# Scratch tensors of a recurrent attention kernel kept in partition order, and the values of each head part projected next to its weighted sum

## The chip, the cores and the metric

One NeuronCore of one Trainium2 chip runs the whole program. The metric is the device time of one execution in microseconds (us); lower is better. Engines are named as in the profile: PE is TensorE's matmul, PEld is TensorE's weight load, DVE is VectorE, ACT is ScalarE, POOL is GpSimd, SP is SyncE, which here issues the transfers.

## The reference, cut to what matters

Forward and all gradients of a layer: a layer norm, an MLP with a squared relu, and an attention that runs over 64 segments of 32 tokens, each with 8 memory rows in front. The memory that goes into a segment is the attention output of the segment before, so 64 forward steps and then 64 backward steps follow each other and cannot overlap.

```python
def _A_ref(x, mem0, Wq, Wk, Wv, Wo, seg_len):       # x 1x2048x512, 32 heads of 128, 8 memory rows
    mem = mem0
    for s in range(n_seg):                          # seg_len 32
        h = concatenate([mem, x[:, s*seg_len:(s+1)*seg_len]], axis=1)
        q, k, v = einsum('btd,dhe->bhte', h, Wq), ...Wk, ...Wv
        p = softmax(where(mask, einsum('bhqe,bhke->bhqk', q, k) * scale, -1e9))
        o = einsum('bhqk,bhke->bhqe', p, v)
        o = einsum('bhte,hed->btd', o, Wo)
        mem = o[:, :M]                              # the next segment needs this
        outs.append(o[:, M:])
# result: x + A(layernorm(x)) + B(layernorm(x)), and its gradients for grad_out
# ... (layer norm, MLP B and the inputs left out)
```

A segment has 8 + 32 rows. The kernel carries 32 of them (the 8 memory rows and 24 tokens) through the recurrent steps. The other 8 tokens of a segment, whose attention outputs no later segment needs, are projected beforehand and finished in a batched "left" stage of 16 blocks of four segments.

## The kernel before

The program has five stretches, one after the other: MLP and projections of the left rows; 64 forward steps; 16 left blocks; 64 backward steps (four to a block, with extra work at a block's end); the weight gradients ("tail"). The stages hand each other their results through scratch tensors in DRAM. On chip a step's tensors have 128 partitions: four head groups g of 32 rows each. In DRAM most of them were kept by row, with the group inside:

```python
# S 2048, D 512, P 128, DC 4, HG 4 head groups, KH 8 heads each, GW = KH*P = 1024, SEG 32, M 8, NB 16, SPB 4
PARTS = ((0, 3), (3, 3), (6, 2))                       # the heads of a group, in three parts
S_NA = dram.tile([NB, HG, SPB, SEG, 3, GW], BF16, name="S_NA")
S_O = dram.tile([NROW, HD], BF16, name="S_O")
S_G = dram.tile([NROW, 3, HD], BF16, name="S_G")
S_RB = dram.tile([NROW, D], F32, name="S_RB")
# ...
def to_rows(t, r0):
    return t[r0:r0 + 32].rearrange("r (g c) -> g r c", g=HG)

def gather(R, XT, W, ks, first, last):                 # back from heads to 512 columns
    for k in ks:
        for g in range(HG):
            for c in range(DC):
                nc.tensor.matmul(R[32 * c:32 * c + 32, 0:P], lhsT=XT[:, k, g, :],
                                 rhs=W[:, g * KH + k, c * P:(c + 1) * P],
                                 start=(first and k == ks[0] and g == 0),
                                 stop=(last and k == ks[-1] and g == HG - 1), tile_position=(0, 32 * c))

def spill_nat(gTs, r0, copies):                        # a step's gradients of q, k, v to DRAM
    i = 0
    for t, gX in gTs:
        gN = wk.tile([P, GW], BF16, name="gNat", tag="gNat")      # this pool has two buffers of a tag
        for k0 in range(0, KH, 4):
            ps = trp.tile([P, 1024], BF16, name="ps_nat", tag="tr")
            for k in range(4):
                transpose_to(ps[:, k * P:(k + 1) * P], gX[:, k0 + k])
            copies[i % len(copies)](gN[:, k0 * P:(k0 + 4) * P], ps[:, 0:512])
            i += 1
        dma(S_G[r0:r0 + 32, t, :].rearrange("r (g c) -> g r c", g=HG), gN[:])
```

A forward step:

```python
for part in PARTS:
    # ... keys and queries projected, turned, scores, softmax, turned weights ET
for part in PARTS:
    proj(N3[:, 2], hT, Wqkv, 2 * HD, part, act_copy)              # the values, copied out by ACT
R = pbig("ps_R")
for i, part in enumerate(PARTS):
    k0, nk = part
    rs = norm(sts[i], L, Pb, part)
    weigh(ETs[i], rs, ((32, N3[:, 2]), (M, vLs)), part, ON)       # weighted sum of the values
    flip(OT[:, k0:k0 + nk], ON, part, act_copy)
    gather(R, OT, Wo, range(k0, k0 + nk), i == 0, i == len(PARTS) - 1)
Rb = ...                                                          # the next step's memory rows
# ... stores of the step: Rf, Rb, N3 into S_NA, ON into S_O and others
```

The left stage reads back the keys and values of the memory rows, and the backward step ends with its stores:

```python
kvM = ls.tile([P, 2, GW], BF16, name="l_kvM", tag="l_kvM")
dma(kvM[:].rearrange("p t c -> p (t c)"),
    S_NA[b].rearrange("g j r t c -> (g j) r (t c)")[:, 0:M, GW:3 * GW])
# ...
def rest(...):                                   # runs under the next backward step
    dma(to_rows(S_RB, s * SEG), Rf[:])
    dma(to_rows(S_MBB[s], 0), Rb[:])
    spill_nat(((2, gv), (1, gk), (0, gq)), s * SEG, (dve_copy, act_copy))
    if j == 0:                                   # last step of a block
        left_done(b, gkL, gvL)                   # three more gathers and another spill_nat
        finish_back(b)                           # loads S_RB rows back, row arithmetic, output rows
```

## Time and profile before

The median of three runs was 5192.39 us (5183.79 to 5195.74). I cut the profiled execution (span 5179.3 us) at four events: the first scores of the forward, the first use of `l_kvM` in the left stage, the first weight load of `b_QK` in the backward, and the last one; the stage lengths in every table below are first-to-last times of such an event, and the short joints between stages are left out. (The prediction cut the stages at their borders instead, so its levels are a little longer; its differences can be compared.)

| stage | us | PE busy, us | granted clock | DMA share |
|---|---|---|---|---|
| forward | 1043.5 | 901 | 0.97 | 0.39 |
| left | 419.8 | 191 | 0.63 | 0.52 |
| backward | 2073.4 | 1407 | 0.75 | 0.28 |
| after the last backward step | 655.3 | 574 | 0.93 | 0.49 |

These come from the table of stretches of the kernel before. Its columns are the stretch and its length, then busy time and instruction count of PE, PEld, DVE, ACT and POOL, then the granted TensorE clock, the DMA share (of 16 engines) and GB/s.

```profile
882.00:1925.00 1043.00, 901.39 (x25539) 538.59 (x25537) 490.96 (x1710) 443.65 (x1269) 180.39 (x502) 0.97 0.39 127
1986.00:2406.00 420.00, 191.09 (x6630) 127.16 (x6634) 157.63 (x398) 75.25 (x169) 40.97 (x63) 0.63 0.52 158
2451.00:4524.00 2073.00, 1407.09 (x49934) 1089.65 (x49932) 617.64 (x2538) 443.58 (x1575) 69.73 (x106) 0.75 0.28 87
4524.00:5179.00 655.00, 573.86 (x3106) 265.99 (x3094) 7.66 (x22) 80.24 (x145) 3.56 (x3) 0.93 0.49 169
```

In the backward PE is idle for a third of the time and its clock is low. Why it is idle stands in the list of waits of the kernel before over the whole span (engine, line, what it waited for: us in total, times, longest us):

```profile
DVE gNat L383 <- DMA S_G<-gNat: 718.3, 111, 10.7
...
ACT gNat L380 <- DMA S_G<-gNat: 520.2, 98, 9.4
...
PE ps_tr L179 <- DVE gNat L383: 310.1, 48, 8.3
```

The chain of waits in order of time shows one such place in a step (start us, us, what):

```profile
3206.96 0.33 PE ps_nat L179 x4
3207.29 0.13 PE ps_proj L402
3207.42 10.64 DMA S_G<-gNat
...
3218.18 0.43 DVE gNat L383
```

Three stores of a step share two buffers. The copy of the third needs the buffer of the first, and that store is still running; PE stands behind the copy. The same list for PE alone, in the backward (2451 to 4524):

```profile
PE ps_tr L179 <- DVE gNat L383: 310.1, 48, 8.3
PE ps_gR L485 <- issue: 77.8, 86, 2.5
...
PE ps_gkq L509 <- issue: 52.4, 46, 3.5
PE ps_gRL L485 <- issue: 46.0, 32, 2.0
```

"issue" is idle time in which PE waited for nothing that the profile shows: 176.2 us here.

### The profile page before, as it was taken

How to read it: one execution, taken by the hardware profiler on the slowest of the kernel's cores; microseconds unless marked ns; L12 is line 12 of the kernel's file. 1: busy time of each engine (PE TensorE's matmuls, PEld its weight loads, DVE VectorE, ACT ScalarE, POOL GpSimd, SP SyncE). 2: the span in 40 equal slices, each digit the busy share in tenths (PEclk: the TensorE clock that was granted, in tenths of full speed). 3: DMA queues.
4: the chain of work that ended last, by engine and by line, in shares of the span. 5: the costliest groups of instructions: out<-in, count | busy, mean ns of one | idle time of the engine just before them, and what ended most of it. 6: DMA issues, size and time to landing. Idle time of an engine off the chain costs nothing.

```text
span 5179.3 us, 196279 instructions
## 1 busy us (share of the span) xinstructions
PE 3590.4 (69%) x89874; PEld 2270.7 (44%) x89874; DVE 1515.1 (29%) x5110; ACT 1225.2 (24%) x3450; POOL 312.3 (6%) x741
## 2 busy tenths in 40 slices
PE   3940658888888882444666766666666666649999
PEld 1520224555555541322555555555555555524444
DVE  5520003444444442333232332323322233300000
ACT  1310024444444431111222222222222222201111
POOL 0000000111111110000000000000000000000000
PEclk8975989999999995666777777777777877769999
DMA  4377564344433346555222222222222222255553
GB/s 141 121 174 211 164 230 160 123 131 132 133 130 129 126 149 222 154 163 167 81 89 87 88 88 89 88 90 90 90 86 88 89 85 86 71 165 188 193 182 123
DMA packets 457504, 672.89 MB, mean 130 GB/s; under 512 B 159817, under 2 KB 257762, under 8 KB 454370
## 3 DMA queue, kind: packets, MB, share of 16 engines
q1 hardware_dynamic: 456674, 660.34, 40.2%
q8 instruction: 702, 11.50, 0.9%
q14 instruction: 128, 1.05, 0.1%
HBM read 349.84 MB, written 289.94 MB: 124 GB/s over the span
## 4 chain that ended last, share of the span: by engine, by line
PE 53%; DMA 28%; DVE 6%; ACT 5%; issue 4%; SPq 3%; POOL 1%; DVEq 0%; POOLq 0%; ACTq 0%
DMA S_G<-gNat 13%; PE ps_gR L485 11%; PE ps_proj L402 9%; PE ps_gw L953 8%; PE ps_tr L179 5%; PE ps_R L485 4%; PE ps_gwo L966 3%; PE ps_gkq L509 2%; DMA l_kvM<-S_NA 2%; PE ps_wgh L470 2%; DVE ON L475 1%; DMA S_WT<-wtt 1%; ACT OT L380 1%; PE ps_nat L179 1%; PE ps_sc L426 1%
## 5 line engine op out<-in xcount | busy, mean ns | idle before, releaser
L402 PE MATMUL ps_proj<-Wqkv,hT 128*32 128x384 bf16 x9216 | 474.4, 312 | 0.5 <-ACT hT L634 0.3
L383 DVE COPY gNat<-ps_nat 128x512 bf16<-128x512 bf16 x240 | 101.9, 425 | 797.9 <-DMA S_G<-gNat 718.3
L485 PE MATMUL ps_gR<-WT_39551,gk 128*32 128x128 bf16 x8192 | 239.1, 275 | 125.2 <-DVE gk L383 66.1
L953 PEld LDWEIGHTS <-HNc 128*128 128x128 bf16 x1920 | 188.4, 98 | 295.1 <-issue 70.3
L179 PE MATMUL ps_tr<-ident,gON 128*128 128x128 bf16 x512 | 82.8, 294 | 310.7 <-DVE gNat L383 310.1
L380 ACT COPY gNat<-ps_nat 128x512 bf16<-128x512 bf16 x240 | 140.5, 586 | 603.9 <-DMA S_G<-gNat 520.2
L402 PEld LDWEIGHTS <-hT 128*32 128x32 bf16 x9216 | 210.4, 96 | 97.9 <-issue 4.1
L485 PE MATMUL ps_gR<-WT_39549,gv 128*32 128x128 bf16 x8192 | 243.9, 293 | 6.2 <-issue 5.2
L485 PEld LDWEIGHTS <-gk 128*32 128x32 bf16 x8192 | 178.2, 122 | 157.3 <-DVE gk L383 68.5
L380 ACT CAST gk<-ps_gkq 128x192 bf16<-128x192 f32 (+1 forms) x256 | 70.2, 274 | 738.1 <-PE ps_gkq L509 738.1
L402 PE MATMUL ps_proj<-WoT,goT 128*32 128x384 bf16 (+1 forms) x3072 | 205.7, 352 | 23.3 <-POOL goT L799 23.0
L485 PE MATMUL ps_gR<-WT_48287,gq 128*32 128x128 bf16 x8192 | 197.9, 262 | 24.9 <-issue 24.1
L485 PEld LDWEIGHTS <-gv 128*32 128x32 bf16 x8192 | 201.3, 132 | 25.1 <-ACT gv L859 13.6
L383 DVE CAST gk<-ps_gkq 128x192 bf16<-128x192 f32 (+1 forms) x256 | 72.9, 285 | 433.8 <-PE ps_gkq L509 433.7
L485 PE MATMUL ps_R<-Wo,OT 128*32 128x128 bf16 x8192 | 153.9, 231 | 58.7 <-ACT OT L380 55.6
L485 PEld LDWEIGHTS <-gq 128*32 128x32 bf16 x8192 | 172.9, 121 | 35.5 <-issue 34.3
L179 PEld LDWEIGHTS <-gON 128*128 128x128 bf16 x512 | 42.3, 117 | 318.5 <-issue 309.1
L470 PEld LDWEIGHTS <-ET 32*32 32x32 bf16 (+1 forms) x5120 | 84.9, 100 | 193.7 <-issue 184.8
L485 PEld LDWEIGHTS <-OT 128*32 128x32 bf16 x8192 | 128.3, 103 | 84.0 <-ACT OT L380 78.8
L470 PE MATMUL ps_wgh<-l_kvM,ET 32*32 32x128 bf16 x512 | 30.2, 300 | 166.1 <-DMA l_kvM<-S_NA 164.1
L345 PE MATMUL ps_w_2827<-ghn,xnN 128*128 128x512 bf16 x16 | 6.5, 405 | 190.2 <-DMA ghn<-S_GH1N 190.2
L475 DVE TENSOR_TENSOR ON<-ps_wgh,sm_rs 128x384 bf16<-128x384 f32 (+1 forms) x192 | 92.6, 510 | 149.6 <-PE ps_wgh L470 149.5
(952 smaller groups left out, 7047.2 us busy)
## 6 DMA issues: line engine op xcount, KB each, us to landing
S_G<-gNat SPq DMA_DIRECT2D x240, 256.0 KB
b_QK<-S_NA SPq DMA_DIRECT2D x64, 512.0 KB
S_VTA<-vT SPq DMA_DIRECT2D x64, 320.0 KB
b_vT<-S_VTA SPq DMA_DIRECT2D x64, 320.0 KB
S_O<-ON SPq DMA_DIRECT2D x64, 256.0 KB
ghn<-S_GH1N SPq DMA_DIRECT2D x32, 448.0 KB
an<-S_AN SPq DMA_DIRECT2D x32, 448.0 KB
S_WT<-wtt SPq DMA_DIRECT2D x48, 256.0 KB
```

Of the source, the lines that this page charges most:

```text
L179: nc.tensor.transpose(ps_ap, in_ap, ident[base:base + k, base:base + k])
L345: nc.tensor.matmul(pss[k][:, :nf], lhsT=xnN[:, rc, dc * P:(dc + 1) * P], rhs=ghn[:, f0g:f0g + nf], start=(rc == 0), stop=(rc == TC - 1),)
L380: nc.scalar.copy(out, in_)
L383: nc.vector.tensor_copy(out, in_)
L402: nc.tensor.matmul(ps[32 * g:32 * g + 32, 0:nk * P], lhsT=hT[:, dc, :], rhs=W[:, dc, c:c + nk * P], start=(dc == 0), stop=(dc == DC - 1), ...
L426: nc.tensor.matmul(sc3[32 * g:32 * g + 32, k, c:c + n], lhsT=qT[:, k0 + k, g, :], rhs=kT[:, k0 + k, g, :], start=(mask is None), stop=True ...
L470: nc.tensor.matmul(ps[32 * g:32 * g + 32, k * P:(k + 1) * P], lhsT=ET[32 * g:32 * g + n, k, i, :], rhs=V[32 * g:32 * g + n, (k0 + k) * P:( ...
L475: nc.vector.tensor_tensor(out=dst[:, k0 * P:(k0 + nk) * P].rearrange("p (k e) -> p k e", k=nk), in0=ps[:, 0:nk * P].rearrange("p (k e) -> ...
L485: nc.tensor.matmul(R[32 * c:32 * c + 32, 0:P], lhsT=XT[:, k, g, :], rhs=W[:, g * KH + k, c * P:(c + 1) * P], start=(first and k == ks[0] a ...
L509: nc.tensor.matmul(out(ps[g], k), lhsT=N_[32 * g:32 * g + m, k * P:(k + 1) * P], rhs=X(k)[32 * g:32 * g + m], start=first, stop=last, tile ...
L953: nc.tensor.matmul(ps[:], lhsT=HNc[:, rc, dc * P:(dc + 1) * P], rhs=gn[:, rc, u * 512:(u + 1) * 512], start=(rc == 0), stop=(rc == RC_ALL ...
L966: nc.tensor.matmul(ps[:], lhsT=on[:, rc, i * P:(i + 1) * P], rhs=GOc[:, rc, :], start=(rc == 0), stop=(rc == RC_ALL - 1))
```

## The change

There are two independent intents. First, the scratch tensors are stored in partition order, so that both sides of a step's transfer have 128 as their outer dimension. The author counted on transfers spread over more DMA engines, and "the spread" means these layouts. With it, the three stores of a step's gradients become one of 768 KB from a larger tile, with still two buffers (so with two steps of slack); the rows of a block are finished later; two pairs of tiles share a tag to make room. Second, in the forward each part's values are projected directly before the weighted sum that uses them, instead of all three parts before the first.

```diff
-    S_NA = dram.tile([NB, HG, SPB, SEG, 3, GW], BF16, name="S_NA")
+    S_NA = dram.tile([NSEG, HG, SEG, 3, GW], BF16, name="S_NA")
-    S_O = dram.tile([NROW, HD], BF16, name="S_O")
-    S_G = dram.tile([NROW, 3, HD], BF16, name="S_G")
+    S_O = dram.tile([NSL, HG, SEG, GW], BF16, name="S_O")
+    S_G = dram.tile([NSL, HG, SEG, 3, GW], BF16, name="S_G")
     ... (S_MBF, S_MBB, S_RF, S_RB likewise; loads and stores adapted)
-        def spill_nat(gTs, r0, copies):
+        def spill_nat(gTs, sl, copies):
             i = 0
+            gN = wk.tile([P, 3, GW], BF16, name="gNat", tag="gNat")
             for t, gX in gTs:
-                gN = wk.tile([P, GW], BF16, name="gNat", tag="gNat")
     ...
-                dma(S_G[r0:r0 + 32, t, :].rearrange("r (g c) -> g r c", g=HG), gN[:])
+            dma(S_G[sl].rearrange("g r t c -> (g r) t c"), gN[:])
     ...
-            for part in PARTS:
-                proj(N3[:, 2], hT, Wqkv, 2 * HD, part, act_copy)
             R = pbig("ps_R")
             for i, part in enumerate(PARTS):
                 k0, nk = part
+                proj(N3[:, 2], hT, Wqkv, 2 * HD, part, act_copy)
                 rs = norm(sts[i], L, Pb, part)
     ...
-            dma(kvM[:].rearrange("p t c -> p (t c)"),
-                S_NA[b].rearrange("g j r t c -> (g j) r (t c)")[:, 0:M, GW:3 * GW])
+            for g in range(HG):
+                dma(kvM[32 * g:32 * g + 32].rearrange("p t c -> p (t c)"),
+                    S_NA[b * SPB:(b + 1) * SPB, g].rearrange("j r t c -> j r (t c)")[:, 0:M, GW:3 * GW])
     ...
                 if j == 0:
                     left_done(b, gkL, gvL)
-                    finish_back(b)
+                if j == 1 and b < NB - 1:
+                    finish_back(b + 1)
     ... (after the loop: finish_back(0); tags of two tile pairs merged;
         the weight gradients load each block as four quarters)
```

More of the change, by code (lines that the diff above doesn't have):

```diff
@@ L114 @@
     S_XN = dram.tile([S, D], BF16, name="S_XN")
-    S_MBF = dram.tile([NSEG, SEG, D], BF16, name="S_MBF")
-    S_MBB = dram.tile([NSEG, SEG, D], BF16, name="S_MBB")
+    NSL = NSEG + NB
+    S_MBF = dram.tile([NSEG, DC, SEG, P], BF16, name="S_MBF")
+    S_MBB = dram.tile([NSEG, DC, SEG, P], BF16, name="S_MBB")
     S_XNT = dram.tile([P, DC, S], BF16, name="S_XNT")
@@ L131 @@
     S_GQL = dram.tile([NB, P, KH, HG, NL], BF16, name="S_GQL")
-    S_O = dram.tile([NROW, HD], BF16, name="S_O")
-    S_G = dram.tile([NROW, 3, HD], BF16, name="S_G")
-    S_RF = dram.tile([NROW, D], F32, name="S_RF")
-    S_RB = dram.tile([NROW, D], F32, name="S_RB")
+    S_O = dram.tile([NSL, HG, SEG, GW], BF16, name="S_O")
+    S_G = dram.tile([NSL, HG, SEG, 3, GW], BF16, name="S_G")
+    S_RF = dram.tile([NSL, DC, SEG, P], F32, name="S_RF")
+    S_RB = dram.tile([NSL, DC, SEG, P], F32, name="S_RB")
     S_WT = dram.tile([P, 3, H, D], BF16, name="S_WT")
@@ L386, in any_copy @@
         nc.any.tensor_copy(out, in_)
-    def to_rows(t, r0):
-        return t[r0:r0 + 32].rearrange("r (g c) -> g r c", g=HG)
     def make_ops(big, trp, scp, wk, sm):
@@ L521, in spill_nat @@
                         transpose_to(ps[:, k * P:(k + 1) * P], gX[:, k0 + k])
-                    copies[i % len(copies)](gN[:, k0 * P:(k0 + 4) * P], ps[:, 0:512])
+                    copies[i % len(copies)](gN[:, t, k0 * P:(k0 + 4) * P], ps[:, 0:512])
                     i += 1
-                dma(S_G[r0:r0 + 32, t, :].rearrange("r (g c) -> g r c", g=HG), gN[:])
+            dma(S_G[sl].rearrange("g r t c -> (g r) t c"), gN[:])
         return pbig, proj, flip, scores, softmax, norm, turn, weigh, gather, dscores, outer, spill_nat
     def fetch_rows(dst, src, b):
-        dma(dst[:], src[b * P:(b + 1) * P, :])
         for j in range(SPB):
-            r0 = AROWS + b * NL + M * j
-            dma(dst[32 * j:32 * j + M, :], src[r0:r0 + M, :])
+            d3 = dst[32 * j:32 * j + 32, :].rearrange("r (c d) -> r c d", c=DC)
+            dma(d3[M:SEG], src[b * SPB + j].rearrange("c r d -> r c d")[M:SEG])
+            dma(d3[0:M], src[NSEG + b].rearrange("c r d -> r c d")[M * j:M * j + M])
     wo_cm = sb("wo", 1, "right")
@@ L647, in rest @@
                 nc.gpsimd.tensor_copy(TM[:, 1, :, :, lc], vT[:, :, :, 0:M])
-                dma(to_rows(S_RF, s * SEG), Rf[:])
-                dma(to_rows(S_MBF[s], 0), Rb[:])
-                dma(S_NA[b, :, j], N3[:])
+                dma(S_RF[s].rearrange("c r d -> (c r) d"), Rf[:])
+                dma(S_MBF[s].rearrange("c r d -> (c r) d"), Rb[:])
+                dma(S_NA[s].rearrange("g r t c -> (g r) t c"), N3[:])
                 dma(S_VTA[s], vT[:])
                 dma(S_PA[s], Pb[:])
-                dma(to_rows(S_O, s * SEG), ON[:])
+                dma(S_O[s].rearrange("g r c -> (g r) c"), ON[:])
                 if j == SPB - 1:
@@ L701 @@
                 gather(R, OT, Wo, range(k0, k0 + nk), k0 == 0, k0 + nk == KH)
-            dma(to_rows(S_O, AROWS + b * NL), ON[:])
+            dma(S_O[NSEG + b].rearrange("g r c -> (g r) c"), ON[:])
             Rf = ld.tile([P, P], F32, name="l_Rf", tag="l_Rf")
             nc.any.tensor_copy(Rf[:], R[:, 0:P])
-            dma(to_rows(S_RF, AROWS + b * NL), Rf[:])
+            dma(S_RF[NSEG + b].rearrange("c r d -> (c r) d"), Rf[:])
             goT = ld.tile([P, DC, NL], BF16, name="goTL", tag="goTL")
@@ L759, in left_done @@
         def left_done(b, gkL, gvL):
-            gqL = bt.tile([P, KH, HG, NL], BF16, name="gqLb", tag="gqLb")
+            gqL = bt.tile([P, KH, HG, NL], BF16, name="gqLb", tag="acc4")
             dma(gqL[:], S_GQL[b])
@@ L766, in left_done @@
             nc.any.tensor_copy(Rf[:], R[:, 0:P])
-            dma(to_rows(S_RB, AROWS + b * NL), Rf[:])
-            spill_nat(((2, gvL), (1, gkL), (0, gqL)), AROWS + b * NL, (dve_copy, act_copy))
+            dma(S_RB[NSEG + b].rearrange("c r d -> (c r) d"), Rf[:])
+            spill_nat(((2, gvL), (1, gkL), (0, gqL)), NSEG + b, (dve_copy, act_copy))
         def finish_back(b):
@@ L791, in finish_back @@
                                     op0=ALU.add, op1=ALU.mult)
-            gib = bt.tile([P, D], BF16, name="gib4", tag="gib4")
+            gib = bt.tile([P, D], BF16, name="gib4", tag="xnb4")
             dma(gib[:], gflat[r0:r0 + P, :])
@@ L818 @@
             QK = bs.tile([P, 2, GW], BF16, name="b_QK", tag="b_QK")
-            dma(QK[:].rearrange("p t c -> p (t c)"), S_NA[b, :, j].rearrange("g r t c -> g r (t c)")[:, :, 0:2 * GW])
+            dma(QK[:], S_NA[s].rearrange("g r t c -> (g r) t c")[:, 0:2, :])
             kLs = bs.tile([P, GW], BF16, name="b_kLs", tag="b_kLs")
@@ L907, in rest @@
             def rest(s=s, b=b, j=j, gv=gv, gk=gk, gq=gq, Rb=Rb, Rf=Rf, gkL=gkL, gvL=gvL):
-                dma(to_rows(S_RB, s * SEG), Rf[:])
-                dma(to_rows(S_MBB[s], 0), Rb[:])
-                spill_nat(((2, gv), (1, gk), (0, gq)), s * SEG, (dve_copy, act_copy))
+                dma(S_RB[s].rearrange("c r d -> (c r) d"), Rf[:])
+                dma(S_MBB[s].rearrange("c r d -> (c r) d"), Rb[:])
+                spill_nat(((2, gv), (1, gk), (0, gq)), s, (dve_copy, act_copy))
                 if j == 0:
                     left_done(b, gkL, gvL)
-                    finish_back(b)
+                if j == 1 and b < NB - 1:
+                    finish_back(b + 1)
             later.append(rest)
@@ L916 @@
             f()
+        finish_back(0)
     bw_cm.__exit__(None, None, None)
-    dma(out2flat[:, :], S_MBB[0][0:M, :])
+    dma(out2flat.rearrange("r (c d) -> r c d", c=DC), S_MBB[0].rearrange("c r d -> r c d")[0:M])
     with tc.tile_pool(name="p5", bufs=2) as p5, tc.tile_pool(name="p5b", bufs=1) as p5b, \
@@ L925, in slot_side @@
             dma(t_[:, 0:TC, :], src.rearrange("(c p) d -> p c d", p=P))
-            sv = smem[:].rearrange("(b j) r d -> j r b d", j=SPB)
+            sv = smem[:].rearrange("(b j) c r d -> j c r b d", j=SPB)
             for j in range(SPB):
@@ L930, in slot_side @@
                 b0, b1 = max(0, -o), min(NB, NB - o)
-                dma(t_[32 * j:32 * j + M, b0:b1, :], sv[jj, 0:M][:, b0 + o:b1 + o, :])
+                for c in range(DC):
+                    dma(t_[32 * j:32 * j + M, b0:b1, c * P:(c + 1) * P], sv[jj, c, 0:M][:, b0 + o:b1 + o, :])
             if lo < 0:
@@ L942 @@
         GOc = slot_side("GOc", gflat, S_MBB, zeros_bf[:], 1)
-        CW = 1024
+        CW = GW
         for t, outW in enumerate((out_3, out_4, out_5)):
@@ L947 @@
                 gn = p5.tile([P, RC_ALL, CW], BF16, name="gn5", tag="gn5")
-                dma(gn[:], S_G[:, t, c0:c0 + CW].rearrange("(c p) n -> p c n", p=P))
+                for j in range(SPB):
+                    dma(gn[32 * j:32 * j + 32], S_G[:, c0 // CW, :, t, :].rearrange("(b j) r c -> j r b c", j=SPB)[j])
                 for dc in range(DC):
@@ L961 @@
             on = p5.tile([P, RC_ALL, CW], BF16, name="on5", tag="gn5")
-            dma(on[:], S_O[:, c0:c0 + CW].rearrange("(c p) n -> p c n", p=P))
+            for j in range(SPB):
+                dma(on[32 * j:32 * j + 32], S_O[:, c0 // CW].rearrange("(b j) r c -> j r b c", j=SPB)[j])
             for i in range(CW // P):
```

## The prediction

> **What bounds it now.** The table of engines by stretch gives: MLP and left projections to 880 us; 64 forward steps, 1077 us (PE busy 911, granted clock 0.96); 16 left blocks, 466 (PE 199, clock 0.62); 64 backward steps, 2147 (PE 1434, clock 0.75); weight gradients, 609 (PE 555). The chain of waits puts 13% (690 us) on stores S_G<-gNat, all in the backward: 8 to 10 us a step, 6 more per block, and 6 to 7 us for an S_RB load. The list of waits agrees: DVE 718, ACT 520 us before gNat. Three 256 KB stores share two gNat buffers; the third waits for the first. Backward DMA is busy 0.29 of 16 engines: as if under five did all.
>
> [...]
>
> **Removed.** (a) [...]S_G becomes one 768 KB store per step with two steps of slack: its waits vanish. (b) A block's gradient rows are finished two steps later, off the chain: 6.5 us load plus 5 us POOL/DVE per block. Replaying one step (3076.8 to 3105.4 us) with its durations in the new instruction order, the first scores start near 3082.0, not 3089.6: 21 us instead of 28.6; the block-end step 32 instead of 45. That is 96 us per block, not 133. Without 6 us gaps PE's clock should rise from 0.75 towards 0.9 ([...]the clocks above agree), counted as 7 us: 89. PE's "issue" gaps inside gathers (176 us) stay. 16 x 44 = 700 us, plus 28 for four stacked stores at the end.
>
> **Added.** (c) Forward: PE's built order is now wgh0, turn, gather0, values 1, wgh1, values 2, turn, wgh2, gather1, turn, gather2; before, all values preceded wgh0, and wgh1/wgh2 followed gather0. PE now stands for the value copy (0.48 us ACT) before wgh0 and wgh1, and the last turn waits for a late wgh2. Replayed from the last scores to Rb: 7.5 us before, 9.8 now; ON0 still waits for DVE's softmax, so the move hides nothing. 2.3 x 64 = 145 us. (d) Left stage: kvM becomes four loads with an outer 4[...]. (e) 24 more small loads before the weight gradients: +12.
>
> **Prediction.** 5190 - 700 - 28 + 145 + 75 + 12 = about 4695 us; 8 in 10: 4480 to 4900. Faster by over 2%: 0.96; within 2%: 0.03; slower: 0.01.
>
> **What would show it.** S_G<-gNat gone from the chain and from DVE's and ACT's waits; backward near 1430 us at clock 0.85 to 0.92. Forward near 1220, PE waiting on ACT's value copy at wgh. Left stage near 540, l_kvM wait near 240.
>
> **What would make it wrong.** If issue gaps grow once no store wait hides them, the backward gains less (4900); if crowded DMA engines cause them, they shrink (4480). If the clock does not rise: +110. [...]If the forward's clock falls with its density, (c) grows.

The sum came to 5190 - 700 - 28 + 145 + 75 + 12 = 4694, about 4695 us. Without (d) the sum would be about 4620 us. The rise of the clock in (b) stands as the estimate from the clocks of the stages above: 0.62 where PE was busy for 199 of 466 us, 0.75 at 1434 of 2147, 0.96 at 911 of 1077. The 28 us of the stores at the end and the 12 us of (e) are estimates too; one of these loads takes 0.42 us to issue in the kernel after (median on SyncE).

## The result, and the profile after

| | before | after |
|---|---|---|
| median, us | 5194.07 (5183.79 to 5198.28, 4 runs) | 5069.13 (5066.16 to 5072.19, 4 runs) |
| span of the profiled run, us | 5179.3 | 5068.2 |
| granted clock, whole span | 0.820 | 0.844 |

The ratio is 0.9762 (95% interval 0.9745 to 0.9779): faster by 2.4%, where 9.6% was predicted, and outside the range. A ratio here and below is the mean time of one kernel's fast runs over that of the other's in the same rounds, so it is not quite the ratio of the quoted medians.

By stage, from first-to-last times of the same events:

| stage, us | before | after | difference | predicted |
|---|---|---|---|---|
| forward | 1043.5 | 1293.2 | +249.7 | +145 |
| left | 419.8 | 455.9 | +36.1 | +75 |
| backward | 2073.4 | 1666.0 | -407.4 | about -700 |
| after the last backward step | 655.3 | 672.4 | +17.1 | -16 (-28 and +12) |
| start and joints | | | -6.6 | 0 |

The sum is -111.1 us, the difference of the two spans. The table of stretches of the kernel after, columns as before, in the same order of stages:

```profile
886.00:2179.00 1293.00, 1045.46 (x25547) 585.44 (x25543) 486.35 (x1711) 463.78 (x1269) 180.65 (x502) 0.89 0.30 103
2237.00:2693.00 456.00, 203.65 (x6630) 131.13 (x6634) 158.00 (x397) 75.19 (x168) 41.23 (x63) 0.62 0.47 147
2730.00:4396.00 1666.00, 1347.29 (x49945) 1023.93 (x49944) 614.64 (x2540) 449.89 (x1576) 70.02 (x106) 0.85 0.34 107
4396.00:5068.00 672.00, 568.47 (x3030) 261.02 (x3078) 7.62 (x22) 81.48 (x145) 3.57 (x3) 0.95 0.78 164
```

The list of waits over the whole span, kernel after. The copies into `gNat` now wait for PE and no longer for a store:

```profile
DVE gNat L385 <- PE ps_nat L181: 308.9, 239, 11.6
...
ACT gNat L382 <- PE ps_nat L181: 140.9, 234, 1.6
```

So the store waits were really taken away, and the backward's clock did rise from 0.75 to 0.85. What PE waits for in the backward (2730 to 4396) is now led by lines that name no releaser:

```profile
PE ps_gR L484 <- issue: 114.5, 134, 2.4
PE ps_gkq L508 <- issue: 76.9, 59, 2.6
PE ps_gRL L484 <- issue: 49.5, 33, 3.4
```

These "issue" gaps grew from 176.2 to 240.9 us. They are not scattered. Here are the gaps of one backward step in PE's timeline, kernel after (start us, us, engine, line, instruction, output and inputs, count, then the idle time before it and its releaser):

```profile
3329.94 3.15 PE L484 MATMUL ps_gR<-WT_39549,gv 128*32 128x128 bf16 x109 [0.86 <-issue]
...
3333.96 0.17 PE L508 MATMUL ps_gkq<-gST,b_QK 32*128 32x32 bf16 x1 [0.47 <-issue]
...
3337.98 1.44 PE L484 MATMUL ps_gR<-WT_39551,gk 128*32 128x128 bf16 x45 [1.71 <-issue]
...
3342.00 0.59 PE L484 MATMUL ps_gR<-WT_48383,gq 128*32 128x128 bf16 x13 [0.41 <-issue]
```

The four starts lie 4.02 us apart. Counting the rows of the trace between them gives exactly 128 products each time, and every product comes with one weight load, so 256 PE instructions. That count does not depend on what the instructions are: the four gaps fall in front of different lines and tiles. Over the whole backward of this trace 232 idle times of PE over 0.15 us end with "issue", and each of the 231 distances between neighbours is a multiple of 128 products (up to two records missing in the trace).

What comes after every 256 instructions is, by three numbers, the supply of instructions itself: the period of 256; the line of an instruction queue on the page of the kernel after (shown below: packets, MB, share of 16 engines), with 702 packets and 11.50 MB, 16 KB each; and 702 times 256 = 179,712, against PE's 89,874 products and as many weight loads (179,748; that count is from the kernel before, and the queue's line has the same packets in both kernels). That the line is PE's shows in two runs below: e7, with some 45,400 PE instructions fewer, has 525 packets, 177 fewer, and e5, with some 7,200 more, has 731. So below, a block is 256 PE instructions, and a refill is the coming of the next one, as these numbers suggest. In the backward of this kernel the refills cost idle time. Where two such gaps follow each other after just one block, the median distance of their ends is 3.75 us (139 distances in the kernel after, mean 3.87, 10th to 90th percentile 3.47 to 4.30; 70 in the kernel before, median 3.74, mean 3.76, 3.47 to 4.02). That is about 68 PE instructions per us.

```profile
q8 instruction: 702, 11.50, 1.0%
```

From this follows a limit that the prediction did not have. The backward stretch holds 49,945 + 49,944 = 99,889 PE instructions, 390 blocks. At 3.75 us each that is 1463 us (an estimate worked out from the two numbers). The prediction's 700 us of gain amount to 2073 - 700 = 1373 us in this cut: below the limit. The limit is not in force all the time: the 139 blocks with a starved gap at both ends take 538 of the 1666 us, and the stage as a whole takes 4.27 us a block.

### The profile page after: what moved, and what is told of

It is laid out like the page before. It is cut to its first block, busy times and chain, and to the rows that moved or that the text cites. A ratio compares the mean times of both kernels' runs of the same rounds, so it can differ in the third digit from the quotient of the medians.

```text
span 5068.2 us, 195611 instructions
## 1 busy us (share of the span) xinstructions
PE 3680.1 (73%) x89788; PEld 2250.3 (44%) x89874; DVE 1507.3 (30%) x5110; ACT 1253.2 (25%) x3450; POOL 313.2 (6%) x741
## 3 DMA queue, kind: packets, MB, share of 16 engines
q8 instruction: 702, 11.50, 1.0%
## 4 chain that ended last, share of the span: by engine, by line
PE 59%; DMA 14%; issue 8%; DVE 8%; ACT 8%; SPq 3%; POOL 0%; ACTq 0%; POOLq 0%; DVEq 0%
PE ps_proj L401 11%; PE ps_gR L484 11%; PE ps_gw L956 7%; PE ps_tr L181 5%; PE ps_R L484 4%; PE ps_nat L181 3%; PE ps_gkq L508 3%; PE ps_gwo L970 3%; DMA l_kvM<-S_NA 2%; PE ps_gRL L484 2%; PE ps_wgh L469 2%; DVE ON L474 2%; ACT OT L382 2%; DMA S_WT<-wtt 1%; DMA ghn<-S_GH1N 1%
## 5 line engine op out<-in xcount | busy, mean ns | idle before, releaser
L401 PE MATMUL ps_proj<-Wqkv,hT 128*32 128x384 bf16 x9216 | 569.0, 349 | 0.6 <-ACT hT L581 0.3
L401 PEld LDWEIGHTS <-hT 128*32 128x32 bf16 x9216 | 223.1, 103 | 127.7 <-issue 36.9
L469 PEld LDWEIGHTS <-ET 32*32 32x32 bf16 (+1 forms) x5120 | 113.3, 104 | 315.1 <-issue 296.3
L484 PE MATMUL ps_gR<-WT_39549,gv 128*32 128x128 bf16 x8192 | 205.3, 255 | 29.0 <-issue 27.9
L484 PE MATMUL ps_R<-Wo,OT 128*32 128x128 bf16 x8192 | 170.7, 238 | 75.8 <-ACT OT L382 75.4
L484 PEld LDWEIGHTS <-gv 128*32 128x32 bf16 x8192 | 164.0, 115 | 44.4 <-issue 37.5
L469 PE MATMUL ps_wgh<-l_kvM,ET 32*32 32x128 bf16 x512 | 41.2, 299 | 192.3 <-DMA l_kvM<-S_NA 190.3
L508 PEld LDWEIGHTS <-b_QK 32*128 32x128 bf16 x4096 | 123.3, 93 | 93.6 <-issue 68.0
L382 ACT COPY OT<-ps_tr 128x384 bf16<-128x384 bf16 (+1 forms) x192 | 85.2, 444 | 212.2 <-PE ps_tr L181 208.2
```

Of the source, the lines that this page charges most:

```text
L382: nc.scalar.copy(out, in_)
L401: nc.tensor.matmul(ps[32 * g:32 * g + 32, 0:nk * P], lhsT=hT[:, dc, :], rhs=W[:, dc, c:c + nk * P], start=(dc == 0), stop=(dc == DC - 1), ...
L469: nc.tensor.matmul(ps[32 * g:32 * g + 32, k * P:(k + 1) * P], lhsT=ET[32 * g:32 * g + n, k, i, :], rhs=V[32 * g:32 * g + n, (k0 + k) * P:( ...
L508: nc.tensor.matmul(out(ps[g], k), lhsT=N_[32 * g:32 * g + m, k * P:(k + 1) * P], rhs=X(k)[32 * g:32 * g + m], start=first, stop=last, tile ...
```

## The experiments

Four questions were open. Is the backward now bound by the supply of PE instructions, or by the array and its clock? Was it the old layout of the stores or the wait for a buffer that cost the backward so much? Is the forward's loss the new order alone? And is the left stage's loss the `kvM` load? All experiments ran beside the kernel before on the same chip, in three groups. In the group of e1 to e4 its median was 5142.26 us (5134.98 to 5147.6), in that of e5 to e8 5167.38 (5159.26 to 5171.23), in that of e9 to e12 5187.49 (5177.78 to 5205.92), seven runs each. e4, e5 and e12 have one run each, whose state is unknown; their stage lengths are read for large differences only. Each row of the table is one profiled execution. The backward's code is the same in after, e1, e5 and e8, and its length there is 1632 to 1683 us, so a difference under some 50 us between two backwards is not read. Stage lengths of all runs, us:

| kernel | forward | left | backward | end | ratio to before |
|---|---|---|---|---|---|
| before | 1043.5 | 419.8 | 2073.4 | 655.3 | 1 |
| after | 1293.2 | 455.9 | 1666.0 | 672.4 | 0.976 |
| e1: after, values first | 1079.4 | 458.5 | 1632.1 | 669.1 | 0.934 |
| e2: before, values moved | 1294.0 | 418.1 | 2061.2 | 653.1 | 1.052 |
| e3: before, four buffers | 1039.9 | 419.6 | 1693.4 | 649.7 | 0.929 |
| e4: after, narrow gather | 1287.8 | 459.7 | 1706.6 | 672.1 | one run, 5087.01 us |
| e5: after, filled waits | 1235.8 | 459.9 | 1682.7 | 674.0 | one run, 5025.6 us |
| e6: after, old S_NA | 1293.7 | 406.9 | 1669.8 | 671.7 | 0.972 |
| e7: after, wide gather | 1294.6 | 463.7 | 1348.1 | 674.1 | 0.920 |
| e8: after, values between | 1021.8 | 452.7 | 1650.9 | 670.7 | 0.923 |
| e9: old layouts, rest of the change | 1043.6 | 418.1 | 1704.8 | 647.8 | 0.924 |
| e10: e9, wide, between | 1042.2 | 415.1 | 1521.1 | 645.2 | 0.889 |
| e11: e6, wide, between | 1019.3 | 401.1 | 1368.6 | 672.5 | 0.859 |
| e12: after, stores twice | 1293.8 | 455.8 | 1760.5 | 681.2 | one run, 5173.76 us |

### e1, e2: the order of the values alone

e1 takes the new order out of the kernel after; e2 puts it alone into the kernel before.

```diff
 # e1, on the kernel after (e2 is the reverse, on the kernel before)
+            for part in PARTS:
+                proj(N3[:, 2], hT, Wqkv, 2 * HD, part, act_copy)
             R = pbig("ps_R")
             for i, part in enumerate(PARTS):
                 k0, nk = part
-                proj(N3[:, 2], hT, Wqkv, 2 * HD, part, act_copy)
                 rs = norm(sts[i], L, Pb, part)
```

> The changed kernel with the forward's value projections all before the first weighted sum again, as before the change; all DRAM layouts of the change kept. Theory A (the moved projections cost the forward, 1062 us before, 1314 us changed; half by the waits of the new order, half by the lower clock those waits bring): the forward falls back to 1050-1080 us at granted clock about 0.96, and the whole run to 4800-4840 us. Rival B (the forward got slower by the new stores' layout): the forward stays above 1250 us and the total within 1% of 5069 us.

> The kernel before with only the value projections moved next to their weighted sum. Theory A: the forward grows by about 250 us to about 1310 us at clock about 0.88, total about 5440 us, the other stages as before. Rival B (layout): forward within 20 us of 1062 us, total within 1% of 5194 us. If only the waits of the order counted, as predicted, and not the clock: forward about 1210 us, clock 0.96.

e1, correct: 4804.23 us (4783.67 to 4824.64, 4 runs), ratio 0.9344 [0.9313, 0.9375]; the forward falls to 1079.4 us. e2, correct: 5408.19 us, ratio 1.0522 [1.0503, 1.0542]; the forward is 1294.0 us, +250 on layouts that were not touched. So the loss of the forward comes with the order of the values and not with the layouts: e2 has all of it on the old ones (the 36 us that e1 keeps over the kernel before are taken up under e9). Its clock falls with it; the forward stretches of e1 and then e2, columns as before:

```profile
875.00:1954.00 1079.00, 920.58 (x25539) 546.91 (x25531) 491.30 (x1711) 443.72 (x1269) 176.97 (x502) 0.95 0.36 123
```

```profile
873.00:2167.00 1294.00, 1046.06 (x25535) 585.59 (x25527) 487.25 (x1713) 463.10 (x1269) 181.80 (x502) 0.88 0.33 102
```

The same 25,535 products take PE 1046 us where they took 901 before: this is a slower clock, not only a longer wait. One step of the kernel after shows how that comes about. PE's idle times in it, from its timeline:

```profile
1504.46 0.23 PE L469 MATMUL ps_wgh<-N_21798,ET 32*32 32x128 bf16 x4 [0.39 <-ACT N_21798 L382]
...
1505.82 0.34 PE L181 MATMUL ps_tr<-ident,ON 128*128 128x128 bf16 x3 [0.65 <-DVE ON L474]
1506.73 1.22 PE L484 MATMUL ps_R<-Wo,OT 128*32 128x128 bf16 x48 [0.57 <-ACT OT L382]
...
1509.80 0.29 PE L469 MATMUL ps_wgh<-N_21798,ET 32*32 32x128 bf16 x4 [0.57 <-ACT N_21798 L382]
...
1514.74 0.28 PE L181 MATMUL ps_tr<-ident,ON 128*128 128x128 bf16 x2 [0.53 <-DVE ON L474]
```

`N` is the value tile: PE now stands for ACT's copy of it before a weighted sum, as predicted. And the same step in stretches (columns as before):

```profile
1504.00:1507.00 3.00, 1.40 (x49) 0.97 (x52) 1.43 (x7) 1.42 (x4) 0.96 (x3) 1.00 0.00 0
1507.00:1510.40 3.40, 2.83 (x84) 1.89 (x72) 0.00 (x0) 0.48 (x1) 0.00 (x0) 0.51 0.09 29
1510.40:1513.60 3.20, 3.13 (x82) 2.03 (x75) 0.56 (x1) 0.85 (x2) 0.61 (x2) 0.50 0.24 102
1513.60:1517.00 3.40, 1.98 (x64) 1.22 (x53) 0.72 (x2) 0.82 (x3) 0.00 (x0) 0.96 0.81 255
```

In the 3 us before 1507 PE is busy for 1.40 us, in short pieces; then the granted clock is 0.51 and 0.50 for 6.6 us, in which PE is nearly always busy, with work that takes up to twice as long: the groups of four `ps_wgh` products start 0.06 us apart from 1504.5 us on, at a clock of 1.00, and 0.11 us apart from 1509.9 us on. No single idle time in the step exceeds 0.65 us, so the clock fell here without any long gap. At which density of work it falls, no run shows.

### e5: the forward's waits filled with products that nobody reads

If the clock follows density, useless products in the waits should make the step shorter although work is added.

```diff
 # e5, on the kernel after
+        def fill(ps, n):
+            for _ in range(n):
+                nc.tensor.matmul(ps[:, 384:512], lhsT=ident[:], rhs=ident[:], start=True, stop=True,
+                                 skip_group_check=True)
...
                 weigh(ETs[i], rs, ((32, N3[:, 2]), (M, vLs)), part, ON)
+                fill(R, 14 if i < 2 else 8)
                 flip(OT[:, k0:k0 + nk], ON, part, act_copy)
+                fill(R, 7)
```

> The changed kernel, with idle spots of PE in the forward (after each weighted sum, after each turn, before the second and third weighted sum) filled by 128x128 products into unused columns of ps_R that nobody reads: some 64 more products a step, 3.7 us of array time. Theory F (of the 3.9 us that the moved values cost per step, about 2.3 are waits of the order and the rest is PE's clock, which the waits push to half speed): a forward step falls from 20.3 us to 18 to 19.3 us, granted clock from 0.88 to above 0.96, although work was added. Rival G (all of it is waiting in the new order): the step stays at 20.3 us or grows.

Correct; 5025.6 us in a single run (state unknown). The forward stretch, columns as before:

```profile
880.00:2116.00 1236.00, 1149.34 (x29129) 732.12 (x29122) 487.41 (x1714) 463.95 (x1270) 181.34 (x502) 1.00 0.31 108
```

The clock is 1.00 throughout and the forward is 57 us shorter, with 3,582 products more (some 56 a step). So a part of the loss is the clock. I had expected a larger gain: a quiet step took 19.56 us instead of 20.3, where 18 to 19.3 had been named. (The 3.7 us of array time for 64 products fit the trace of the kernel after, where each further product of a turn adds 0.06 us at a clock of 1.00: two take 0.28 us, three 0.34.) The filling lies on the chain itself in some places, so 57 us understates the clock's share. A better look is the part of a step that has neither a reordered instruction nor a filling, from Rb to the last scores of the next step: its mean is 8.63 us before (clock 0.99), 9.48 after (0.89) and 8.54 in e5 (1.00).

### e8: the values of the next part projected into the wait of this one

```diff
 # e8, on the kernel after
+            proj(N3[:, 2], hT, Wqkv, 2 * HD, PARTS[0], act_copy)
             R = pbig("ps_R")
             for i, part in enumerate(PARTS):
                 k0, nk = part
-                proj(N3[:, 2], hT, Wqkv, 2 * HD, part, act_copy)
                 rs = norm(sts[i], L, Pb, part)
                 weigh(ETs[i], rs, ((32, N3[:, 2]), (M, vLs)), part, ON)
+                if i + 1 < len(PARTS):
+                    proj(N3[:, 2], hT, Wqkv, 2 * HD, PARTS[i + 1], act_copy)
+                if i > 0:
+                    gather part i - 1
                 flip(OT[:, k0:k0 + nk], ON, part, act_copy)
-                gather part i
+            gather the last part
```

> The changed kernel with another place for the values: the next part's values projected right after a weighted sum, before its turn, and each gather one part later, so PE has work while ON and OT are made. The built order is wgh0, values 1, turn, wgh1, values 2, gather0, turn, wgh2, gather1, turn, gather2. Worked out from the step's durations: 1.0 to 1.5 us shorter than the 16.07 us of a quiet step before, so a step of 14.6 to 15.3 us at clock above 0.95, forward 950-990 us between its first and last scores (1293 in the changed kernel, 1079 with all values first), total ratio to before about 0.91 to 0.92.

Correct: 4767.28 us, ratio 0.9231 [0.9218, 0.9245]. The forward is 1021.8 us, 271 us less than after and 22 us less than before. The intent of moving the values (to give PE work while ON is computed) works if the values come one part ahead. The step was expected at 14.6 to 15.3 us and took 15.96: my expectation was too good, as PE was already busy for 13.86 of 16 us in a step of the kernel before, so little more was to be had.

### e3: four buffers, nothing else

This tells whether the old stores' layout or the wait for a buffer was the cost.

```diff
 # e3, on the kernel before
-                gN = wk.tile([P, GW], BF16, name="gNat", tag="gNat")
+                gN = wk.tile([P, GW], BF16, name="gNat", tag="gNat0" if t == 0 else "gNat")
```

> The kernel before with four gNat buffers instead of two (the third store of a step has its own pair)[...]. Theory C (only the wait for a buffer cost; what remains is PE's supply of instructions, 256 per 3.5 to 4.3 us when it runs dry): the gNat waits nearly vanish and the backward falls from 2130 to 1700-1800 us, about what the whole change got there, total 4770-4880 us. Rival D ([...]the spread was needed): the wait moves to other DMA (QK loads, S_RB) and the backward stays above 1950 us.

Correct: 4779.68 us (4773.42 to 4781.93), ratio 0.9292 [0.9277, 0.9308]. One line, with the old layouts and the stores untouched, gains three times as much as the whole change, which carries the forward's loss. The waits of the copies into `gNat` for a store fall from 1238 us (718.3 and 520.2 above) to 98. Its backward stretch, columns as before:

```profile
2437.00:4130.00 1693.00, 1322.78 (x49915) 1007.07 (x49918) 611.63 (x2540) 449.80 (x1576) 69.88 (x106) 0.85 0.33 106
```

It is 1693 us, 27 above the kernel after and 61 above e1 (the same backward code as after), at about the same clock. So most of the backward's gain came from the slack in buffers; the new layout of the stores was hardly needed for it.

### e4: a quarter of the array work, the same number of instructions

If the array or its clock bounds the backward, streaming 32 instead of 128 columns per gather product must help. If the instruction supply does, nothing changes.

```diff
 # e4, on the kernel after, backward only; gives a wrong result on purpose
+                    n = P if edge or not narrow else 32        # edge: first and last product
-                        nc.tensor.matmul(R[32 * c:32 * c + 32, 0:P], lhsT=XT[:, k, g, :],
-                                         rhs=W[:, g * KH + k, c * P:(c + 1) * P],
+                        nc.tensor.matmul(R[32 * c:32 * c + 32, 0:n], lhsT=XT[:, k, g, :],
+                                         rhs=W[:, g * KH + k, c * P:c * P + n],
```

> The changed kernel with the backward's gathers streaming 32 columns instead of 128 in all but the first and last products of each sum: the same instructions in the same order, a quarter of the array's work in 30,000 of them. Gives a wrong result on purpose. Theory C (instruction supply): backward within 6% of 1706 us (1600 to 1710), the issue gaps grow from about 243 us to above 400 us. Rival E (array time at the granted clock): each gather product drops by some 10 to 20 ns, backward below 1450 us, the gaps unchanged.

Wrong (relative error 0.84 in one of the outputs); 5087.01 us in one run. Backward stretch and PE's waits in it (2707 to 4413):

```profile
2707.00:4413.00 1706.00, 1153.49 (x49933) 810.79 (x49934) 611.15 (x2539) 452.75 (x1575) 70.04 (x106) 0.64 0.32 105
```

```profile
PE ps_gR L486 <- issue: 274.9, 179, 3.1
PE ps_gkq L511 <- issue: 137.9, 63, 3.1
PE ps_gRL L486 <- issue: 66.5, 32, 3.9
```

PE's busy time falls by 194 us (some 6.5 ns for each of the 30,000 products; the rival's 10 to 20 are an estimate, and three quarters of the 29 ns that a gather product takes in the step traced above, 109 in 3.15 us, would be 22) and its issue gaps grow by 238 us; the stage is no shorter (1706.6 against 1666.0). The 203 one-block distances between gap ends have a median of 3.74 us. The array's work was not what the backward waited for. The clock fell to 0.64; what that cost alone cannot be read here, because the array had less work at the same time.

### e7: the same work in fewer, wider instructions

The reverse: keep the arithmetic of the gather and cut its instruction count. One product of 512 columns replaces four of 128; the four head groups are left in four strips of partitions and summed by four small products with a matrix of zeros and ones.

```diff
 # e7, on the kernel after, backward only
             for k in ks:
                 for g in range(HG):
-                    for c in range(DC):
-                        nc.tensor.matmul(R[32 * c:32 * c + 32, 0:P], lhsT=XT[:, k, g, :],
-                                         rhs=W[:, g * KH + k, c * P:(c + 1) * P], ...)
+                    nc.tensor.matmul(R[32 * g:32 * g + 32, :], lhsT=XT[:, k, g, :], rhs=W[:, g * KH + k, :],
+                                     start=(first and k == ks[0]), stop=(last and k == ks[-1]),
+                                     tile_position=(0, 32 * g))
+        def fold(R, one):
+            Rs = one.tile([P, D], BF16, name="Rs", tag="Rs")      # copied by ACT and DVE, half each
+            ...
+            for c in range(DC):
+                nc.tensor.matmul(R2[32 * c:32 * c + 32, 0:P], lhsT=sel[:], rhs=Rs[:, c * P:(c + 1) * P],
+                                 start=True, stop=True, tile_position=(0, 32 * c))
```

> The changed kernel, with the backward's gathers in a quarter of the instructions: each head group has its own column group and streams 512 columns, and the four partial sums are folded by four products with a 0/1 matrix. The same array work, 576 PE instructions fewer in each of 64 steps and 576 fewer in each of 16 block ends, 1 us more latency a step (copy and fold). Theory C (instruction supply, 256 per 3.5 to 4 us, is the backward's limit): a step loses 2.25 refills, some 6 to 8 us, the backward falls from 1666 to 1150-1350 us, issue gaps from 240 us to under 80 us. Rival E (array time and latency are the limit): the backward stays within 60 us of 1666 us or grows by the fold. Results agree with the reference within its tolerance (partial sums rounded to bf16 once).

Correct: 4749.07 us, ratio 0.9201 [0.9168, 0.9235]. Backward stretch and PE's waits in it (2730 to 4078):

```profile
2730.00:4078.00 1348.00, 1237.62 (x27551) 665.33 (x27552) 642.13 (x2618) 475.23 (x1653) 69.96 (x106) 0.98 0.40 130
```

```profile
PE ps_R L507 <- ACT Rs L503: 29.0, 63, 0.5
...
PE ps_gR L488 <- issue: 1.9, 5, 0.7
PE ps_gkq L530 <- issue: 1.3, 3, 0.5
```

The issue gaps are gone (3.2 us), although the fold adds a new wait of its own on the chain (29.0 us in all). The backward is 318 us shorter than after, at clock 0.98. Its 55,103 PE instructions are 215 blocks, 807 us at 3.75 us each, so the supply is no limit any more. The gaps are 238 of the 318 us; PE's busy time fell by 110 us as well (fewer weight loads and a higher clock, not separated), and its other short waits grew. And 1348 us is below the 1373 that the prediction amounts to in this cut: with the limit removed, the stage gets to where the replay of the step had put it, though without the gaps that the replay had kept. (This is a different gather, so it does not prove the replay.) e4 and e7 together show the cause: less array work with the same instructions gained nothing, the same array work with fewer instructions gained 318 us, and the gaps, always whole blocks of 256 instructions apart, went away.

### e12: is the supply slowed by crowded DMA?

The prediction left open whether crowded DMA engines cause the issue gaps. Here every gradient store is done a second time, to a scratch tensor that nobody reads.

```diff
 # e12, on the kernel after
             dma(S_G[sl].rearrange("g r t c -> (g r) t c"), gN[:])
+            dma(S_G2[sl].rearrange("g r t c -> (g r) t c"), gN[:])
```

> The changed kernel with each 768 KB store of a step's gradients done twice (the second into a tensor nobody reads). Theory C in its strict form (a refill of 256 PE instructions takes 3.5 to 4 us whatever else the DMA moves): backward within 2% of 1666 us, issue gaps within 20% of 240 us. Rival J (crowded DMA engines slow the refill): issue gaps above 320 us and backward above 1730 us.

5173.76 us, correct, one run (state unknown). PE's waits in the backward (2730 to 4491):

```profile
PE ps_gR L485 <- issue: 175.3, 138, 3.0
PE ps_gRL L485 <- issue: 71.7, 39, 4.2
PE ps_gkq L509 <- issue: 48.0, 49, 2.7
```

The gaps are 295.0 us instead of 240.9, the backward 1760.5 instead of 1666.0 us (+5.7%). That is outside what the strict theory allowed; of the rival's two marks the backward passed its one and the gaps fell short of 320. The distance of one block has a median of 3.76 us as in the kernel after (3.75), but a mean of 4.01 (3.87 after; 3.72 to 3.88 in before, after, e1, e3, e6 and e9) and a 90th percentile of 4.84 (4.30). No copy into `gNat` waits for one of the doubled stores. So this run speaks for ordinary traffic stretching some refills; it is one run, and of its 94.5 us 54 are gaps and 38 are a longer busy time of PE at a lower clock (0.81). How much of the 3.75 us is a fixed latency was not tested.

### e6: the old form of S_NA

```diff
 # e6, on the kernel after
-    S_NA = dram.tile([NSEG, HG, SEG, 3, GW], BF16, name="S_NA")
+    S_NA = dram.tile([NB, HG, SPB, SEG, 3, GW], BF16, name="S_NA")
     ... (its store, the kvM load and the QK load as in the kernel before)
```

> The changed kernel with S_NA alone in its old layout[...]. If the four kvM loads of the change cost (predicted +75 us, measured between first and last l_kvM use +36 us): the left stage falls by 30 to 40 us, the backward stays within 30 us of 1666 us[...], total 0.5 to 1% under the changed kernel. Rival: the left stage got longer by its small S_RF loads; then it stays.

Correct: 5023.5 us, ratio 0.9721 [0.9698, 0.9744]. PE's wait for `kvM` in the left stage, in the list of waits of before, after and e6, in this order:

```profile
PE ps_wgh L470 <- DMA l_kvM<-S_NA: 164.1, 15, 12.7
```

```profile
PE ps_wgh L469 <- DMA l_kvM<-S_NA: 190.3, 60, 9.7
```

```profile
PE ps_wgh L469 <- DMA l_kvM<-S_NA: 149.3, 15, 11.6
```

The left stage falls from 455.9 to 406.9 us, by 49 where 30 to 40 were expected, and below the kernel before; the backward does not mind that the QK load is back on its old form (1669.8 against 1666.0). The loss of the left stage is this load's, as predicted, at half the predicted size.

### e9, e10, e11: what the layouts are worth

e9 is the change without its layouts and without the new order: one larger tile for the gradients with two buffers, stored by three transfers in the old layout, the finish deferred in the source, the merged tags.

```diff
 # e9, on the kernel before
+            gN = wk.tile([P, 3, GW], BF16, name="gNat", tag="gNat")
             for t, gX in gTs:
-                gN = wk.tile([P, GW], BF16, name="gNat", tag="gNat")
     ...
-                dma(S_G[r0:r0 + 32, t, :].rearrange("r (g c) -> g r c", g=HG), gN[:])
+                dma(S_G[r0:r0 + 32, t, :].rearrange("r (g c) -> g r c", g=HG), gN[:, t, :])
     ...
-                    finish_back(b)
+                if j == 1 and b < NB - 1:
+                    finish_back(b + 1)
 # e10 = e9 + the forward of e8 + the gather of e7
 # e11 = e6 + the forward of e8 + the gather of e7
```

> Of the change only two things kept: gNat as one tile for a step's three stores (two of them), and the gradient rows of a block finished two steps later. All DRAM layouts[...] and the values' place as before the change. Theory H (the spread[...] bought nothing, the wait for gNat and the late rows were all): backward 1590-1680 us between first and last QK use (1632 with the spread), forward about 1040 us, left stage about 420 us, ratio to before 0.91 to 0.93, at or under the 0.934 of the kernel with the spread and values first. Rival D[...]: backward above 1750 us, ratio above 0.945.

> The kernel of the run before with the wide gathers in the backward and the values projected between the weighted sums. If instruction supply is what the backward of every kernel so far met, the wide gather saves some 300 us here too: backward 1300-1400 us, ratio to before 0.84 to 0.865. If [...]PE is faster (a block in 84 us instead of 104): gNat or QK waits return and the backward stays above 1450 us.

> The changed kernel with S_NA in its old layout, wide gathers in the backward, values between the weighted sums. Sum of the single gains measured (270 us for the values, 318 us for the gather, some 30 us for S_NA): ratio to before 0.845 to 0.87; backward near 1350 us. The spread shows its worth here if anywhere: faster than the old layouts by more than 1%[...].

All three are correct. e9: 4796.28 us, ratio 0.9242 [0.9219, 0.9266]. e10: 4615.57 us, ratio 0.8891 [0.8858, 0.8925]. e11: 4457.27 us (4453.11 to 4466.23), ratio 0.8592 [0.857, 0.8614]; it beats both kernels.

Two expectations of the backward were missed: e9 lies above 1590 to 1680, and e10 above 1450, where its rival had put it, though by another wait than the two named. Against e1 (everything new but the order), e9 is worse in the backward by 73 us (1704.8 against 1632.1) and better in the left stage by 40 and at the end by 21 us; in the forward it is better by 36 us, but with the interleaved order the new layouts are 20 us faster (e8 1021.8, e10 1042.2), so the layouts' part in the forward stays open. As long as PE starves for instructions, the new layout is worth nearly nothing in sum. In e10 and e11 PE no longer starves (0.8 us of issue gaps in e10's list; in e11 PE is busy for 1253 of 1368 us), and now the layouts are worth 152 us in the backward (1521.1 against 1368.6). What comes up in e10 is a late load of rows from `S_RB`, behind which POOL, then DVE's copies and then PE stand. From the lists of PE's waits in the backward, e9 (2449 to 4154) and then e10 (2450 to 3900, short of its end at 3976):

```profile
...
PE ps_gR L485 <- DVE gk L383: 81.0, 15, 6.7
```

```profile
PE ps_gR L489 <- DVE gk L387: 149.9, 14, 11.7
```

The count of 14 or 15 shows that it happens once in a block. Over e10's whole backward this wait is 160.0 us, in e11 14.0, so it makes nearly all of the 152 us. Why the load comes late was not taken apart. In e11 the same stage runs at a granted clock of 0.97.

## Why the prediction was right or wrong

The direction was right; the size was wrong: 4695 us predicted, 5069 measured. The terms, in the prediction's letters:

- **(a) and (b), the backward: predicted about -700 us, measured -407. This is the step that failed.** What it says of the waits came true: no copy into `gNat` waits for a store, PE no longer waits behind the late rows, and the clock rose from 0.75 to 0.85. The failing sentence is "PE's "issue" gaps inside gathers (176 us) stay", with the 89 us per block that stands on it (measured: 105 us from one block to the next). The gaps were taken for a fixed cost to be carried over. They are the mark of a rate: 256 PE instructions per 3.75 us or so. PE's 390 blocks of instructions need about 1463 us at that rate, more than the 1373 that was predicted in this cut, so by this estimate taking waits away could not help below that. Instead the gaps grew, 176 to 241 us, as the prediction's own list of dangers had it ("If issue gaps grow once no store wait hides them"), only with too small a cost. e4 and e7 show it. The replay itself was too short as well, and the prediction's own numbers could have said so: PE's busy time before, 1407 us, less 7 us a block for the clock, plus the 176 us of gaps that were to stay, is 1471 us, 98 above 1373. The other parts of the 293 us that are missing: PE's busy time fell by 60 us and not by 112 (52), the gaps grew (65), and PE has 78 us of other, mostly short waits. What a faster clock gave, the gaps took back.
- **(b), the deferred rows: the wait went, but not by the deferral as far as the runs show.** In the traces of before, e9 and after alike the rows' first operation runs in the second step after a block's last; the built order is not the source's. Within that step it is the 17th DVE instruction before, the 22nd in e9 and the 28th after. PE's wait behind it (`ps_gR` for DVE's `gk`, 66 us before) is 81.0 us in e9, which has the deferral and the old layouts, and gone in the kernel after.
- **(c), the forward: predicted +145, measured +250.** The mechanism (PE standing for the value copy, a late last weighted sum) is in the timeline, and e2 has all of it with the order alone. From the last scores to Rb the median step takes 10.2 us at a full clock, where 7.5 were measured before and 9.8 were predicted: the order itself cost 2.7 us a step where 2.3 was predicted, some 170 of the 250 us. (The step traced above is a slow one, 12.5 us, because the half clock falls into this part of it.) The term that was left out is the clock: it fell from 0.97 to 0.89, which the prediction named as a danger but did not cost. By difference some 80 us are left for it; e5, at full clock, shows at least 57.
- **(d), the left stage: predicted +75, measured +36.** The load is the cause (e6 takes it back, and more), the size is half: the wait for `l_kvM` grew by 26 us (164.1 to 190.3), not by 75. The measured growth is 26 / 16 = 1.6 us of wait per block. The estimate behind the 75 us rested on the number of DMA engines of a load, which was not shown; why the four loads take longer than the one stays open.
- **(e) and the stores at the end: predicted -16, measured +17.** The loads of the weight gradients, now in quarters, hold the DMA engines at a share of 0.78 instead of 0.49 for about the same GB/s. The table of stages places it: the end takes 645 to 655 us in every run with the old layouts and 669 to 681 in every one with the new (671.7 in e6, where `S_NA` alone is old). Which of the layouts or loads it is, no run took apart.

Summed up: the backward fell short by 293 us, the forward by 105, the end by 33; the left stage gave back 39 and the joints 7. That is 385 us, against 374 between the medians; the rest is that spans and medians are different runs.

The reading of the DMA engines deserves a word. The prediction took the old stores for slow because few engines carry them. That was not shown: no view shows single engines. What the trace of the kernel before shows is a share of 0.28 of 16 engines in the backward (the work of 4.5, an estimate from the share) and a store of 256 KB that landed 10.6 us after its issue. But that a store is slow does not say that it has to be made fast: e3 left it as it was and gave it two buffers more, and got 380 of the 407 us in the backward.

## What to carry to other kernels

When a wait is taken away, ask what rate stands behind it: count an engine's instructions in the stage, and if "issue" gaps recur after a fixed number of instructions, suspect a supply limit; here (256 instructions, 3.75 us) fewer and wider instructions moved it (e7, 318 us less) and less array work did not (e4, 1706.6 us against 1666.0). Before trusting a replayed step, add up the engine's busy time and the idle time that is to stay: the forecast must not lie below the sum. Before making a slow store fast, try more buffers for it (two more gave 380 of the 407 us here); and before moving work on PE to sit next to its use, see whether the copy out and the pieces of idle time that it makes will lower the clock: here a project-one-ahead order had the intended effect (e8, 0.99 in the forward) and the project-beside order the opposite (0.89, from 0.97). Changes of layout that are worth nothing while another limit holds can be worth 150 us once that limit is gone, so test them again then.
